# Talking-heads attention and a squared-ReLU FFN on one core: where the first batch's loads of v and w_in stand in the load queue

## The chip, the cores and the metric

The kernel runs on one core of a Trainium2 chip. The metric is the device time of one execution in microseconds (us), taken as the median over runs. Beside it there is one profiled execution, whose trace gives every instruction with its start, its length and what it waited for. The engines go by short names: PE is TensorE (PEld its weight loads), DVE is VectorE, ACT is ScalarE, POOL is GpSimd and SP is SyncE. SP computes nothing here; it issues transfers.

## The reference

Attention over 8 batches, 12 heads, 448 positions and a head dimension of 64, with the heads mixed before and after the softmax, and then a feed-forward net over all 3584 tokens:

```python
scores = scale * np.matmul(q, k.transpose(0, 1, 3, 2))
scores = np.einsum('bhij,hg->bgij', scores, w_pre)
scores = scores - np.max(scores, axis=-1, keepdims=True)
attn = np.exp(scores)
attn = attn / (np.sum(attn, axis=-1, keepdims=True) + 1e-09)
attn = np.einsum('bhij,hg->bgij', attn, w_post)
attn_out = np.matmul(attn, v)
x = attn_out.transpose(0, 2, 1, 3).reshape(B * S, H * D)      # 3584 x 768
out = np.maximum(x @ w_in, 0.0) ** 2 @ w_out                   # d_ff = 2048
```

The inputs are float32. They are turned into bfloat16 on their way into the core's memory, by the transfers that POOL issues.

## The kernel before

**The stages of a batch.** q and k come in by head and are transposed (line 491; the last 64 positions of q, the tails, at line 519). A score (line 629) is the product of one pair of heads with one of four blocks of rows: block 0 holds the tails, blocks 1 to 3 hold 128 rows each. The scores are cast into one of two buffers `snat`, in turn (lines 395 and 397). Mixing the heads needs them in another layout, with ten positions times twelve heads on the partitions, so SP issues a relayout (`move`, line 658), a transfer from `snat` to a small tile `sch`. In the first batch some relayouts carry three chunks at once (`triple`, line 607) into tiles that lie in `osb` and `h2`, which the feed-forward net needs only later (`tri`, line 387); two chunks share a smaller tile `schl`.

A chunk is then: mix with w_pre (line 753, or 749 with three matmuls for a chunk of a triple), row maximum on DVE (758), exponential with its sum on ACT (761), reciprocal (767), scaled w_post on POOL (770, `wq`), mix back and transpose (777), and a copy into `atb`. There are 45 chunks to a batch, 360 in all. The product with v (817) fills the rows of x; two batches make a unit's columns for the feed-forward net (870 with w_in, 883 ReLU, 886 square, 902 with w_out, 917 and 926 out).

**The order of the work.** The order of the instructions on every engine is written once, by a planner in the kernel (`Planner`, line 101). Each operation has a priority: chunk n has priority n, and its score and relayout have n less `AHEAD` (lines 636 and 670). The planner walks a model of the engines and of two transfer queues, "LOAD" for what POOL issues and "DMA" for what SP issues, and emits what is ready with the smallest priority. On the chip each engine then runs its instructions in this order and waits only for what the data needs. The planner lets a load be issued only when the seventh load before it has landed in its model (line 414). The constants AHEAD, LAST_W1, W2_AT and Q1_AT set places in the order.

**The loads of the first batch.** Ahead of the planner the kernel issues eight loads for k, the tails and q (LOADS0, line 53). Then, in `first_batch` (line 1022), POOL has a small copy, `hold` (line 1036), which reads a few columns of `snat` 0, and so waits until the six casts of the tails' scores are done. Behind it POOL issues v in two halves (`load_half`, line 1001) and six tiles of w_in (`load_w1`, line 987). The tiles of w_out and q and k of the next batch are issued at fixed chunks (lines 1049 to 1052). The product with v comes at 52 us and the first matmul with w_in at 57 us.

Of the kernel before, what the change touches and what calls it, by code (L numbers as in the profile page):

```python
# [10 lines left out]
BF16 = mybir.dt.bfloat16  # L11
F32 = mybir.dt.float32

B, H, S, D = 8, 12, 448, 64
DMODEL = H * D
DFF = 2048
NPAIR = H // 2
# [22 lines left out]
PIECE = NPAIR // 2  # L40
NE = 6
NSCH = 11
AHEAD = 7.4
FIFO = 50
ROWS, COLS = 1, 2
TURN = 95
# [27 lines left out]
TRI_IN = (0, 1)  # L74
W2_AT = [18, 21, 24, 27]
Q1_AT = [13, 16]
LAST_W1 = 4
TAIL0, Q0 = 19, 0.7
EARLY0 = 0

# [20 lines left out]
class Planner:  # L101
# [7 lines left out]
    def add(self, eng, ns, pri, fn, deps=(), lat=60, bank=None, frees=None, mode=0):  # L109
        op = Op(eng if isinstance(eng, dict) else {eng: ns}, lat, pri, fn, list(deps), bank, frees, mode)  # L110
        self.ops.append(op)
        return op
# [158 lines left out]
def kernel(  # L271
# [11 lines left out]
    nc = tc.nc  # L283
    P = nc.NUM_PARTITIONS

    sb = ctx.enter_context(tc.tile_pool(name="sb", bufs=1))
# [9 lines left out]
    vs = sb.tile([P_KEYS, H, NB, D], BF16, name="vs")  # L296
# [32 lines left out]
    def load_kv(dst, src, b, h0, h1):  # L329
        nc.gpsimd.dma_start(  # L330
            out=dst[:, h0:h1, :, :].rearrange("p h r d -> p h (r d)"),
            in_=src[b, h0:h1].rearrange("h (p r) d -> p h (r d)", r=NB),
        )
# [3 lines left out]
    for what in LOADS0:  # L337
# [15 lines left out]
        out=smask[:, :], in_=ident[0:KC, 0:KC].rearrange("p (s h) -> p s h", s=CI), axis=AX.X, op=ALU.add,  # L353
    )
    wmix = many(3, "wmix", [KC, P], BF16)
    for t_ in wmix:
# [4 lines left out]
        out=nmask[:, :], in0=smask[:, :], scalar1=-SCALE, scalar2=1.0, op0=ALU.mult, op1=ALU.mult,  # L361
# [3 lines left out]
        out=perm[:, :].rearrange("k (s x p) -> k s x p", s=CI, x=2),  # L365
        in_=ident[0:KC, 0:KC].rearrange("k (s p x) -> k s x p", s=CI, x=2),
    )
    for t_ in wmix[1:]:
        nc.vector.tensor_tensor(
            out=t_[:, 0:KC].rearrange("p (s h) -> p s h", s=CI),  # L370
# [4 lines left out]
        out=wback[:, :, :], in0=wpost_rep[:, :].unsqueeze(2).to_broadcast([KC, H, CI]),  # L375
# [5 lines left out]
        out=keep_m[:, :], in_=ident[0:KC, 0:KC].rearrange("p (s m g) -> p m s g", s=CI, m=3), axis=AX.XY, op=ALU.add,  # L381
# [19 lines left out]
    add = pl.add  # L401
# [12 lines left out]
    def load(rows, each, pri, fn, deps):  # L414
        if len(loads) >= 7:
            deps = list(deps) + [loads[-7]]
        op = add("POOL", 750, pri, fn, deps, lat=850)
        done = pl.moved("LOAD", rows, each[0], each[1], 0, [op], 1500)
        loads.append(done)
        return done  # L420

    q_in, k_in, v_in = {}, {}, {}
# [43 lines left out]
    score_ops, scopy = {}, {}  # L466
# [12 lines left out]
    def t_qk(b, p):  # L479
        i, at_ = slot_of(b, p)  # L480
        pri = b * NCHUNK - 19 + 1.5 * p
        old = used(b, p // PIECE)

        def turn(tag, at, ins, src, blocks, rows, dve, act, put):
            key = (tag, "t", b, p, blocks)

            def mms(slot):
                v_ = slot[:, :].bitcast(BF16)
                for r in range(blocks):
                    for x in range(2):  # L490
                        nc.tensor.transpose(  # L491
                            v_[64 * x:64 * x + 64, r * rows:(r + 1) * rows], src[:, 2 * p + x, r, :],
                            ident[0:rows, 0:rows],
                        )

            mm = add("PE", 200 + 55 * blocks, at, keep(key, mms), ins + old, lat=200, bank=key)
            ev = add({"DVE": dve, "ACT": act}, 0, at, lambda eng: put(eng, slots[key][:, :].bitcast(BF16)), [mm], frees=key)
            return mm, ev

        def put_k(eng, v_):  # L500
            copy(eng, kt[i][:, :, at_, :], v_[:, 0:S].rearrange("p (j c) -> p j c", c=P_KEYS))

        def put_q(eng, v_):
            copy(eng, qz[i][:, :, at_, :], v_[:, 0:NJ * P].rearrange("p (r c) -> p r c", c=P))

        mk, ek = turn("g", pri, [k_in[b, p // 2]], ks, NB, P_KEYS, 340, 460, put_k)
        at = pri + Q0 if b == 0 else pri + 3
        mq, eq = turn("g", at, [q_in[b, p // 2]], qs, NJ, P, 300, 420, put_q)
        ready[b, p] = [[ek]] + [[ek, eq]] * NJ
        got_op[b, p] = [mk, mq]  # L510

    def t_tail(b, g):
        key = ("f" if b == 0 else "g", "z", b, g)
        old = [score_ops[b - 1, 0, p] for p in range(3 * g, 3 * g + 3)] if b > 0 else []

        def mms(slot):
            v_ = slot[:, :].bitcast(BF16)
            for i in range(3):
                nc.tensor.transpose(v_[:, i * P:(i + 1) * P], qt[:, 3 * g + i, :], ident[:, :])

        def put(eng):
            copy(
                eng, zt[:, 3 * g:3 * g + 3, :].rearrange("p a c -> p (a c)"),
                slots[key][:, :].bitcast(BF16)[:, 0:3 * P],
            )

        pri = b * NCHUNK - (19 if b > 0 else TAIL0) + 3 * g
        mm = add("PE", 200, pri, keep(key, mms), [tail_in[b]] + old, lat=200, bank=key)
        ev = add({"DVE": 360, "ACT": 440}, 0, pri, put, [mm], frees=key)
        got_tail.setdefault(b, []).append(mm)  # L530
        for p in range(3 * g, 3 * g + 3):
            ready_tail[b, p] = ev
# [63 lines left out]
    def flip(b, r):  # L596
        return 1 - r if b == 0 and r < 2 and EARLY == 0 else r
# [4 lines left out]
    def store_of(b, r):  # L602
        return snat[flip(b, r) % 2]
# [9 lines left out]
    def groups(b, r):  # L613
        size = GROUP if b >= GROUP_AT and r > 0 else 1
        return [range(p, p + size) for p in range(0, NPAIR, size)]

    def score(b, r, group):
# [13 lines left out]
        first = [0, EARLY, C0[2], C0[3]][r] if b == 0 else C0[r]  # L631
        pri = b * NCHUNK + first - AHEAD - 0.6 - (0.7 if r == 0 else 1.4) * (NPAIR - p)
        n = b * (NJ + 1) + r - 2
# [19 lines left out]
    def block_of(c):  # L653
        r = sum(c >= c0 for c0 in C0) - 1
        return r, c - C0[r]
# [8 lines left out]
    def relayout(b, c):  # L664
# [6 lines left out]
        deps = list(scopy[b, r]) + (list(scopy[b, r - 1]) if r == 1 and cc == 0 else [])  # L671
        pri = n - AHEAD
        if r == 2 and cc == 0:
# [295 lines left out]
    started = add("POOL", int(1000 * at_) + 700, -100, lambda: None)  # L969
# [14 lines left out]
    w1_in, later = [], {}  # L984
    w2_in = [add("W2", 0, 0, lambda: None, lat=0) for i in range(4)]

    def load_w1(c2, pri, more=()):
        w1_in.append(load(16, (152, 148), pri, lambda: nc.gpsimd.dma_start(
            out=w1[c2][:, :], in_=moe_w_in[c2 * 128:(c2 + 1) * 128, 0:DFF], max_dma_last_dim=4096,
        ), [started, *more]))  # L990

    def load_w2(f4, n):
        f_, c_ = 8 * (f4 % 2), 384 * (f4 // 2)
# [3 lines left out]
        ), gate(n))  # L997
        done.next.append(w2_in[f4])
        w2_in[f4].left += 1

    def load_half(b, n, x, deps):
        h0 = x * H // 2
        v_in[b].append(load(42, (46, 58), n, lambda: load_kv(vs, v, b, h0, h0 + H // 2), deps))

    def load_v(b, n, deps):
        v_in[b] = [load(42, (46, 58), n, lambda h0=h0: load_kv(vs, v, b, h0, h0 + H // 2), deps) for h0 in (0, H // 2)]
# [14 lines left out]

    def first_batch():
        for i in range(NPAIR):
            if i == 0:
                v_in[0] = []
                for x in range(0):
                    load_half(0, -30 + x, x, [started])
        for p in range(NPAIR):
            t_qk(0, p)
        for g in range(2):  # L1030
            t_tail(0, g)
        for r in (1, 0):
            for p in groups(0, r):
                score(0, r, p)
        hold = sb.tile([P, NPAIR], BF16, name="hold")
        opened = add("POOL", 150, -6, lambda: nc.gpsimd.tensor_copy(
            out=hold[:, :], in_=store_of(0, 0)[:, 0:NPAIR, 0],
        ), scopy[0, 0])
        for x in range(0, 2):
            load_half(0, -5 + 0.1 * x, x, [opened])  # L1040
        for i in range(NPAIR):
            load_w1(i, -4 + 0.1 * i, [opened])
        for n, c in enumerate(ORDER0):
            if c in C0[2:]:
                for p in groups(0, block_of(c)[0]):
                    score(0, block_of(c)[0], p)
            relayout(0, c)
            chunk(0, c)
            if n in W2_AT:
                load_w2(W2_AT.index(n), n)  # L1050
            if n in Q1_AT:
                load_ahead(1, n, 6 * Q1_AT.index(n))
            if c == C0[1]:
                for g in range(3):
                    av(0, 0, g, 0, P_ROWS)
                unit(0, 0)
            if c == C0[2]:
                for g in range(3):
                    av(0, 0, g, P_ROWS, XA)
            if c == C0[3]:  # L1060
                for g in range(3):
                    av(0, 1, g, 0, P_ROWS)
                unit(0, 1)
        for g in range(3):
            av(0, 1, g, P_ROWS, XB)
        unit(0, 2)
# [78 lines left out]
```

## Time and profile before

| what | value |
|---|---|
| median of 3 runs | 590.29 us (589.7 to 591.21) |
| profiled execution | 591.14 us, of which 589.4 us are the span |
| PE busy | 565.2 us, 96% of the span |
| DVE / ACT / POOL busy | 82% / 80% / 55% |
| transfers issued by POOL and SP | 82.33 MB, mean 140 GB/s |
| w_in's six tiles, 512 KB each | median 21.8 us from issue to landing |
| granted TensorE clock, mean | 0.99 |

The span is the time between the first and the last instruction of the profiled execution. A line of the timeline gives the start, the length, the engine, the line in the kernel, what is written and read, how many instructions are merged, and in square brackets how long the engine stood idle before it and which instruction or transfer ended that. A window gives the busy time of each engine in a stretch, the granted clock (1.00 is full), the busy share of the core's sixteen DMA engines (over 1 where transfers overlap on an engine) and the bytes per second. A line of the chain of waits gives the start, the length and the work of one link; the chain is followed back from the last instruction.

### The profile page before, as it was taken

To read this page: it belongs to the slowest core of one execution; us is meant where nothing else is said; L and a number is where in the kernel's file an instruction comes from. 1 tells how busy PE (TensorE), PEld (TensorE's weight loads), DVE (VectorE), ACT (ScalarE), POOL (GpSimd) and SP (SyncE) were. 2 spreads that over 40 slices of the span, in tenths; PEclk is the share of its full clock that TensorE was granted. 3 is DMA by queue.
4 is the path that set the end of the run, shared out by engine and by line. 5 is a ranking of instruction groups with operands and counts; after the bars stand their busy time and mean duration, and the time that the engine had idled before them with its cause. 6 is when DMAs were issued, how large, how long until landed. Compare 5 with 4: busy or idle time off the path is not lost.

```text
span 589.4 us, 17018 instructions
## 1 busy us (share of the span) xinstructions
PE 565.2 (96%) x5751; PEld 403.8 (69%) x5751; DVE 486.1 (82%) x1240; ACT 471.3 (80%) x1239; POOL 326.2 (55%) x600
## 2 busy tenths in 40 slices
PE   5698999999999999999999999999999999999996
PEld 3346766776668766776867776876767866867783
DVE  4697999997798998999898898989798898989201
ACT  4597998888988988989898878888889988788330
POOL 4436647546667437744865538744865624735340
PEclk9897999999999999999999999999999999999999
DMA  8899969984596449964596639974497547322021
GB/s 95 181 217 215 211 135 166 181 168 130 104 203 147 131 127 164 187 152 135 102 187 168 144 90 169 183 142 140 89 175 186 136 107 144 105 83 78 2 53 55
DMA packets 132086, 82.33 MB, mean 140 GB/s; under 512 B 59582, under 2 KB 126286, under 8 KB 131998
## 3 DMA queue, kind: packets, MB, share of 16 engines
q1 hardware_dynamic: 85214, 58.42, 40.6%
q0 software_dynamic: 46784, 22.81, 30.6%
q8 instruction: 45, 0.74, 0.5%
q14 instruction: 43, 0.35, 0.2%
HBM read 45.62 MB, written 11.01 MB: 96 GB/s over the span
## 4 chain that ended last, share of the span: by engine, by line
PE 84%; ACT 5%; DMA 5%; issue 2%; DVE 1%; SPq 1%; POOL 1%; DVEq 0%; POOLq 0%; ACTq 0%
PE bank L902 24%; PE bank L870 24%; PE bank L777 12%; PE bank L753 10%; PE bank L817 7%; PE bank L629 6%; DMA sch<-snat 3%; ACT es L761 2%; DMA osb<-snat 1%; SPq L658 1%; ACT snat L397 1%; ACT hr L883 1%; DVE mn L758 1%; PE bank L491 1%; DMA qt<-in_q_dram 1%
## 5 line engine op out<-in xcount | busy, mean ns | idle before, releaser
L761 ACT ACTIVATE es<-bank,mn 120x448 bf16<-120x448 f32 x360 | 229.4, 643 | 40.2 <-DVE mn L758 35.1
L770 POOL TENSOR_SCALAR wq<-wback,rc 120x120 bf16<-120x120 f32 x360 | 130.5, 367 | 179.4 <-DVE rc L767 104.2
L758 DVE TENSOR_REDUCE mn<-bank 120x1 f32<-120x448 f32 x360 | 209.5, 609 | 8.4 <-PE bank L749 5.2
L902 PE MATMUL bank<-w,h 128*128 128x384 bf16 x896 | 174.3, 325 | 0.9 <-ACT es L761 0.5
L395 DVE CAST atb<-bank 112x480 bf16<-112x480 f32 (+3 forms) x227 | 142.1, 634 | 30.8 <-PE bank L777 27.8
L870 PE MATMUL bank<-xt,w 128*128 128x256 bf16 (+1 forms) x1632 | 164.5, 254 | 0.2
L870 PEld LDWEIGHTS <-w 128*128 128x128 bf16 x1632 | 135.7, 98 | 21.9 <-issue 2.3
L886 POOL TENSOR_TENSOR h<-hr 128x512 bf16<-128x512 f32 x112 | 116.2, 1039 | 54.7 <-ACT hr L883 52.2
L777 PEld LDWEIGHTS <-es 120*112 120x112 bf16 (+1 forms) x1440 | 116.9, 130 | 39.5 <-issue 8.1
L777 PE MATMUL bank<-wq,es 120*112 120x120 bf16 (+1 forms) x1440 | 129.6, 218 | 2.8 <-POOL wq L770 1.9
L902 PEld LDWEIGHTS <-h 128*128 128x128 bf16 x896 | 83.5, 97 | 55.1 <-issue 5.6
L753 PE MATMUL bank<-sch,wmix 120*128 120x448 bf16 x334 | 103.9, 355 | 1.3 <-DMA sch<-snat 0.9
L395 DVE CAST snat<-bank 128x448 bf16<-128x448 f32 x164 | 96.0, 612 | 6.3 <-PE bank L629 3.5
L397 ACT CAST atb<-bank 112x480 bf16<-112x480 f32 (+3 forms) x157 | 82.3, 540 | 15.7 <-PE bank L777 14.2
L883 ACT ACTIVATE hr<-bank 128x512 f32<-128x512 f32 x112 | 67.1, 599 | 31.0 <-PE bank L870 25.2
L397 ACT CAST snat<-bank 128x448 bf16<-128x448 f32 x172 | 84.9, 550 | 4.3 <-PE bank L629 3.2
L761 ACT ACTIVATION_READ_ACCUMULATOR es<-bank,mn 120x1 f32 x360 | 75.7, 210 | 0.0
L767 DVE RECIPROCAL rc<-sm 120x1 f32<-120x1 f32 x360 | 52.7, 153 | 14.4 <-ACT es L761 12.3
L917 DVE COPY osb<-bank 128x384 f32<-128x384 f32 x56 | 30.7, 549 | 31.6 <-PE bank L902 31.3
L753 PEld LDWEIGHTS <-wmix 120*128 120x128 bf16 x342 | 30.3, 98 | 19.0 <-issue 7.8
L629 PE MATMUL bank<-kt,qz 64*128 64x448 bf16 x288 | 42.6, 354 | 0.5 <-ACT atb L397 0.2
L817 PE MATMUL bank<-atb,vs 112*64 112x192 bf16 (+3 forms) x864 | 42.2, 255 | 0.5 <-ACT atb L397 0.5
(57 smaller groups left out, 248.6 us busy)
## 6 DMA issues: line engine op xcount, KB each, us to landing
sch<-snat SPq DMA_DIRECT2D x318, 105.0 KB
out_dram<-osb SPq DMA_DIRECT2D x23, 360.0 KB
vs<-in_v_dram POOLq DMA_DIRECT2D x16, 336.0 KB, 9.6
ks<-in_k_dram POOLq DMA_DIRECT2D x14, 336.0 KB, 10.0
qs<-in_q_dram POOLq DMA_DIRECT2D x14, 288.0 KB, 8.2
w<-in_moe_w_in_dram POOLq DMA_DIRECT2D x6, 512.0 KB, 21.8
w<-in_moe_w_out_dram POOLq DMA_DIRECT2D x4, 768.0 KB, 24.5
out_dram<-osb SPq DMA_DIRECT2D x8, 192.0 KB
```

What stands on the lines that cost most here:

```text
L395: nc.vector.tensor_copy(out=out_, in_=in_)
L397: nc.scalar.copy(out=out_, in_=in_)
L629: nc.tensor.matmul(slot[:, 0:S], lhsT=lhsT, rhs=kt[i][half, :, at_, :], start=True, stop=True)
L753: nc.tensor.matmul(slot[:, 0:S], lhsT=wm[0:rows, :], rhs=src[0:rows, :], start=True, stop=True,)
L758: nc.vector.tensor_reduce(out=mn[i][0:rows, :], in_=slots[mk][0:rows, 0:S], axis=AX.X, op=ALU.min)
L761: nc.scalar.activation(out=es[i][0:rows, 0:S], in_=slots[mk][0:rows, 0:S], func=ACT.Exp, scale=-1.0, bias=mn[i][0:rows, 0:1], accum_out=sm ...
L770: nc.gpsimd.tensor_scalar(out=wq[i][0:rows, :, 0:ns], in0=wback[0:rows, :, 0:ns], scalar1=rc[i][0:rows, 0:1], scalar2=1.0, op0=ALU.mult, o ...
L777: nc.tensor.matmul(slot[0:P_KEYS, jb * H * ns:(jb + 1) * H * ns], lhsT=es[i][0:rows, jb * P_KEYS:(jb + 1) * P_KEYS], rhs=wq[i][0:rows, :, ...
L817: nc.tensor.matmul(v_[64 * hh:64 * hh + 64, i, 0:x1 - x0], lhsT=vs[:, 2 * c2 + hh, jb, :], rhs=atb[half][:, jb, 2 * c2 + hh, x0:x1], start ...
L870: nc.tensor.matmul(slot[:, j * w:(j + 1) * w], lhsT=w1[c2][:, (f0 + j) * 128:(f0 + j + 1) * 128], rhs=xt[:, c2, a:z], start=(c2 == 0), sto ...
L886: nc.gpsimd.tensor_tensor(out=h2_[:, f0:f0 + nf, 0:w], in0=hr[gi % 2][:, :].rearrange("p (f c) -> p f c", f=nf), in1=hr[gi % 2][:, :].rear ...
L902: nc.tensor.matmul(slot[:, 0:384], lhsT=h2_[:, ft, mt * 128:(mt + 1) * 128], rhs=w2[:, ft, nt * 384:(nt + 1) * 384], start=(ft == 0), stop ...
```

## The change

Three things change in the first batch, and one constant changes for all batches.

The gate goes: the copy `hold` and the wait that it carries are taken out, and with it the argument through which loads waited for it. The six tiles of w_in and the two halves of v are made ready by `started` alone, the point at which POOL has issued q. Their order becomes one tile of w_in, both halves of v (`load_v`, which the other batches use already), and then the other five tiles: LAST_W1 says before which tile v stands. AHEAD goes from 7.4 to 7, which moves the priority of every score and relayout by 0.4 chunk.

```diff
-AHEAD = 7.4
+AHEAD = 7
...
-LAST_W1 = 4
+LAST_W1 = 1
...
-    def load_w1(c2, pri, more=()):
+    def load_w1(c2, pri):
         w1_in.append(load(16, (152, 148), pri, lambda: nc.gpsimd.dma_start(
             out=w1[c2][:, :], in_=moe_w_in[c2 * 128:(c2 + 1) * 128, 0:DFF], max_dma_last_dim=4096,
-        ), [started, *more]))
+        ), [started]))
...
-    def load_half(b, n, x, deps):
-        h0 = x * H // 2
-        v_in[b].append(load(42, (46, 58), n, lambda: load_kv(vs, v, b, h0, h0 + H // 2), deps))
...
     def first_batch():
         for i in range(NPAIR):
-            if i == 0:
-                v_in[0] = []
-                for x in range(0):
-                    load_half(0, -30 + x, x, [started])
+            if i == LAST_W1:
+                load_v(0, 0.1 + i, [started])
+            load_w1(i, 0.1 + i)
...
-        hold = sb.tile([P, NPAIR], BF16, name="hold")
-        opened = add("POOL", 150, -6, lambda: nc.gpsimd.tensor_copy(
-            out=hold[:, :], in_=store_of(0, 0)[:, 0:NPAIR, 0],
-        ), scopy[0, 0])
-        for x in range(0, 2):
-            load_half(0, -5 + 0.1 * x, x, [opened])
-        for i in range(NPAIR):
-            load_w1(i, -4 + 0.1 * i, [opened])
```

`load_v`, unchanged, issues the same two transfers as the two calls of `load_half`:

```python
def load_v(b, n, deps):
    v_in[b] = [load(42, (46, 58), n, lambda h0=h0: load_kv(vs, v, b, h0, h0 + H // 2), deps) for h0 in (0, H // 2)]
```

## The prediction

> **What bounds the kernel now.** I read the page's head first, then busy time and clock by windows, the timelines of SP, POOL, PE and DVE over the first 60 us, and the chain of waits. The page:
>
> ```profile
> span 589.4 us, 17018 instructions
> PE 565.2 (96%) x5751; PEld 403.8 (69%) x5751; DVE 486.1 (82%) x1240; ACT 471.3 (80%) x1239; POOL 326.2 (55%) x600
> ```
>
> TensorE (PE) is busy for 96% of the span, so a change far from it costs nothing. The windows show where the rest lies (columns: window, its length, busy time of PE, PEld, DVE, ACT and POOL, granted clock, DMA share, GB/s):
>
> ```profile
> 11.00:12.00 1.00, 1.00 (x18) 0.83 (x18) 1.00 (x4) 0.77 (x2) 0.00 (x0) 1.00 0.70 82
> 12.00:13.00 1.00, 1.00 (x8) 0.30 (x8) 0.81 (x3) 1.00 (x3) 0.00 (x0) 1.00 0.07 8
> 14.00:15.00 1.00, 1.00 (x18) 0.48 (x16) 0.57 (x2) 0.81 (x2) 0.00 (x0) 1.00 0.00 0
> 16.00:17.00 1.00, 0.96 (x7) 0.22 (x8) 1.00 (x5) 1.00 (x4) 1.00 (x2) 1.00 0.23 75
> 24.00:28.00 4.00, 3.67 (x15) 1.93 (x16) 2.01 (x4) 1.38 (x4) 0.36 (x1) 0.57 1.16 271
> 48.00:56.00 8.00, 7.09 (x112) 5.46 (x113) 5.08 (x13) 4.92 (x15) 4.67 (x8) 0.57 1.38 207
> 100.00:540.00 440.00, 438.10 (x4387) 315.81 (x4386) 393.26 (x997) 377.42 (x1004) 253.99 (x476) 1.00 0.73 144
> ```
>
> From 100 to 540 us PE idles for 1.9 us in all. The time to be won or lost by the loads is in the first 60 us. There the DMA lies idle from about 11.7 to 16.2 us, and the granted clock is 0.57 in two stretches. This is the start, by engine:
>
> ```profile
> 15.20 0.19 POOL L1036 COPY hold<-snat 128x6 bf16<-128x6 bf16 x1 [6.87 <-ACT qz L397]
> 15.70 1.59 POOL L330 DMA_DIRECT2D vs<-in_v_dram  x2 [0.30 <-issue]
> 17.27 4.33 POOL L988 DMA_DIRECT2D w<-in_moe_w_in_dram  x6
> 15.15 1.82 SPq L658 DMA_DIRECT2D osb<-snat  x2
> 38.60 0.76 SPq L658 DMA_DIRECT2D schl<-snat  x1
> 19.56 1.86 PE L749 MATMUL bank<-osb,wtri_all 120*128 120x448 bf16 x9 [2.15 <-DMA osb<-snat]
> 24.33 2.31 PE L749 MATMUL bank<-osb,wtri_all 120*128 120x448 bf16 x6 [2.91 <-DMA osb<-snat]
> 25.56 0.62 DVE L758 TENSOR_REDUCE mn<-bank 120x1 f32<-120x448 f32 x1 [3.04 <-PE bank L749]
> 45.65 0.10 PEld L753 LDWEIGHTS <-wmix 96*128 96x128 bf16 x1 [0.75 <-DMA schl<-snat]
> ```
>
> POOL waits until 15.20 for the tails' scores and then issues the eight loads. The first relayout leaves SP at 15.15 and releases chunks 0 to 2 at 19.56, 4.4 us later. The second leaves at 16.05 and releases chunks 3 to 5 only at 24.33, 8.3 us later, because v and w_in came between. VectorE (DVE) idles 3.04 us for it. The last line is the nearest row to what the change makes: the schl relayout, 63 KB, leaves SP at 38.60 when SP's earlier relayouts have landed and tiles of w_in still wait in the load queue. It lands at 45.65, after 7.05 us.
>
> **The change, part by part.**
>
> *The gate goes.* One POOL copy of 0.19 us goes; POOL was idle for 6.87 us before it, so this is worth nothing.
>
> *Eight loads move forward.* They are two for v (1.59 us of POOL together) and six for w_in (4.33 us), 5.9 us of issue. POOL's last work before them ends at 8.34, so they issue from 8.34 to about 14.3 instead of 15.70 to 21.6. On POOL they pass only the gate; the first work behind them is the first wq at 22.35, so POOL costs nothing. On the DMA they now stand ahead of the three relayouts that SP issues at 15.15, 16.05 and 17.02, where they stood beside or behind them. The loads flow from the end of q, 11.7 us, instead of 16.5 to 17: about 5 us of transfer is moved into idle DMA time. One tile of w_in lands about every 2.3 us when little else runs (34.6, then 36.9, in the landings before), half of v took about 2 us at the 160 to 188 GB/s that k and q had. So when the first relayout starts to move at 16.2, one tile and half of v are through, and half of v and five tiles lie ahead.
>
> *The first relayout.* No row shows it behind a full queue, so I bound it. Below: no added wait. Above: all of the schl row's 7.05 us as wait. Between: the second relayout, 8.3 us against 4.4 us, 3.9 us of wait. The schl row, less 4.4 us for a larger transfer with nothing ahead, gives at least 2.65 us. I take 3.9, the nearest in size and place. Chunks 0 to 2 then start at 23.5 instead of 19.56.
>
> The Trainium skill speaks against this step: its page "DMA: Bandwidth & Descriptors", section "Queues, rings and completion order", says that each DMA engine goes round between the queues it has work for and changes at packet boundaries, so a relayout would not stand behind a whole queue of loads. The 7.05 us for 63 KB look longer than such sharing, but do not exclude it. By that page the sum below would be 2.1 - 1.6 = +0.5 us instead of +2.1.
>
> *What that delays.* PE idles from 17.4 to 23.5. After the 2.9 us idle before 24.33 the clock was 0.57 and six matmuls took 2.31 us, 0.385 each; nine of them take 3.5 us, to 27.0. The second relayout stands behind the first in SP's queue; the large ones landed some 1.6 to 2 us apart (24.3 to 32.3 for the next four and three small ones), so it is there by 25.5 and no longer late. Chunks 3 to 5 then run at full clock, nine matmuls of 0.24 us (0.73 us per three later on) and 0.6 us of the matmuls between them, to 29.7. Before, they were through at 28.1. So the start loses **+1.6 us**, with ends of 0 (the first relayout comes early enough for chunk 3) and +4.7 (7.05 us of wait: 3.1 more). The later relayouts of this block follow the same queue: the one issued at 23.88 and landed at 32.34 stands on the chain of waits, and comes 1 to 2 us later, within this term.
>
> ```profile
> 23.88 8.46 DMA osb<-snat
> 41.90 9.38 DMA sch<-snat
> ```
>
> *Earlier end of w_in.* The last tile landed at 48.6 (issued 20.8, 27.8 us) and now lands near 43.6. Its consumer, the first hidden layer, starts at 56.9 both ways. What gains are the relayouts from 38.6 to 45, of which one stands on the chain with 9.38 us. PE itself waited for them twice, 0.9 us in all, at 49.3 and 51.3; VectorE was busy without a gap from 44 to 52, so more than that is not theirs to give. The next batch's q and k still come at 43.5, so I take half, **-0.5 us** (ends 0 and -0.9).
>
> *AHEAD 7.4 to 7.* Scores and relayouts of every batch get a due time 0.4 chunk later: 589.4 us over 360 chunks is 1.64 us per chunk, so 0.65 us. From 100 to 560 us the waits for relayouts are these (total, times, longest):
>
> ```profile
> PEld L753 <- DMA sch<-snat: 1.1, 3, 0.4
> ```
>
> Three loads of weights come late, and each could be 0.65 us later: +2.0 us above. Below, a new order could take away the 1.9 us that PE idles from 100 to 540: -1.9. I take half of the upper end, **+1.0 us**, since the waits that exist can only lengthen and a gain needs luck in the order. LAST_W1 only names the place of v.
>
> The sum is +1.6 - 0.5 + 1.0 = +2.1 us. The profiled execution had a span of 589.4 us and 591.14 us in all, 1.74 around the span; it would become 591.5 and 593.2. The median of the three runs is 590.29, 0.85 under the profiled execution, and becomes 592.4.
>
> **The rivals.** A difference of 0.3%, 1.8 us, is about what a measurement of this kernel can tell from no change.
>
> *Faster: the second clock slump goes.* From 48 to 56 us PE is busy 7.09 us at a mean clock of 0.57; at full clock that work is some 4.1 us, 3.0 less. The slump follows idle PE from 44 to 52 (5.73 of 8 us busy). If the first relayout shares the DMA at once, its 2 us of movement double at most: it lands by 21.6, its nine matmuls are through before 24.33, and the start costs nothing. If the relayouts near 40 then land early enough to keep PE busy, 0.9 + 3.0 go: 586.4 us. It decides when chunks 0 to 2 start before about 21.6 and the clock holds past 48. For it: the DMA idle at 12 to 16 us is truly unused. Against: VectorE is full from 44 to 52, so PE waits there anyhow. The page named above would take its first half so: its round between the queues is that sharing.
>
> *Hidden anyway.* The start costs 0, the later waits give 0.5 to 0.9, the order 0 to +1.0: 589.4 to 590.8. For it: the second relayout already set the start, and its landing need not move.
>
> *The load queue holds more.* If the wait is the whole 7.05 us, the start costs +4.7, and with the upper end for AHEAD the sum is 4.7 + 2.0 = +6.7: 597.0. For it: five whole tiles of w_in lie ahead, and near 38.6 three or four did. Against: at 16.2 half of the near queue is v, whose parts are smaller.
>
> *AHEAD decides.* -1.9 with a start of 0 to +0.5 gives 588.4 to 588.9; the upper side lies within the other cases.
>
> **How the numbers follow.** Forecast with its neighbourhood (590.8 to 594.5) 0.45; the deeper queue (594.5 to 597) 0.17; hidden anyway 0.13; the clock slump gone 0.17; a lucky order 0.08. Faster by over 0.3% (under 588.5) are the last two, 0.25. Within 0.3% are the hidden case and the lower edge of the forecast's neighbourhood, 0.13 + 0.06 = 0.19. Slower is the rest of it, 0.39 + 0.17 = 0.56. The likeliest is 592.4. The range reaches from 587.5, just above the full price of the slump, to 597.0; about 0.1 is left out on each side. The forecast's own range is 590.8 to 594.5.
>
> **What would show it.** Right: POOL issues loads from about 8.3 us without a wait; the DMA moves over 150 GB/s from 12 to 15 us; the first nine matmuls of chunks 0 to 2 start at 22.5 to 25 us, released by the osb relayout; the wait before chunk 3 is gone and its reduction comes at 26.5 to 28 us; the last tile of w_in lands near 44; from 100 to 540 us PE idles 2 to 4 us. Wrong: chunks 0 to 2 start before 21 us (the loads don't hold a relayout up), or the clock stays at 1.0 from 48 to 56, or PE's busy time from 100 to 540 moves by more than 2 us, which would make the order written by the planner, not the loads, the cause.

## The result and the profile after

The changed kernel takes 595.66 us (median of six runs, 594.08 to 597.23) against 590.79 for the kernel before (six runs): a ratio of 1.0081, 95% interval 1.0058 to 1.0104. That is 4.9 us slower. The forecast was slower by 2.1 us. Here and below, a difference in us is the ratio minus one, times the time of the kernel before that was measured beside it. The head of the page after:

```profile
span 594.4 us, 17010 instructions
PE 562.9 (95%) x5751; PEld 401.9 (68%) x5751; DVE 486.7 (82%) x1242; ACT 473.6 (80%) x1243; POOL 322.9 (54%) x593
```

PE's busy time fell by 2.3 us and the span rose by 5.0, so PE idles 31.5 us instead of 24.2. The windows of the kernel after (window, length, busy time of PE, PEld, DVE, ACT, POOL, granted clock, DMA share, GB/s) say where:

```profile
12.00:15.00 3.00, 3.00 (x46) 1.45 (x45) 2.95 (x8) 3.00 (x8) 2.08 (x3) 1.00 1.18 199
19.00:22.00 3.00, 0.00 (x0) 0.00 (x0) 0.00 (x0) 0.00 (x0) 0.00 (x0) 0.50 1.10 276
38.00:42.00 4.00, 3.71 (x28) 1.63 (x28) 4.00 (x11) 3.39 (x8) 0.73 (x2) 1.00 0.02 4
48.00:56.00 8.00, 5.65 (x73) 4.32 (x73) 5.70 (x15) 5.32 (x18) 4.75 (x9) 0.82 1.35 208
100.00:540.00 440.00, 433.50 (x4362) 312.12 (x4361) 392.36 (x996) 379.10 (x1005) 250.10 (x466) 1.00 0.74 144
```

The DMA is now busy from 12 to 15 us, as it was to be, and empty from 38 to 42, where the kernel before was still loading w_in. But the last line holds most of the loss: from 100 to 540 us, far behind the loads, PE idles 6.5 us instead of 1.9. The timeline of the start, by engine:

```profile
8.24 0.76 POOL L988 DMA_DIRECT2D w<-in_moe_w_in_dram  x1
9.00 1.57 POOL L330 DMA_DIRECT2D vs<-in_v_dram  x2
10.54 3.54 POOL L988 DMA_DIRECT2D w<-in_moe_w_in_dram  x5
14.23 1.82 SPq L658 DMA_DIRECT2D osb<-snat  x2
22.16 4.81 PE L749 MATMUL bank<-osb,wtri_all 120*128 120x448 bf16 x15 [5.67 <-DMA osb<-snat]
27.23 0.73 PE L749 MATMUL bank<-osb,wtri_all 120*128 120x448 bf16 x3
23.48 0.62 DVE L758 TENSOR_REDUCE mn<-bank 120x1 f32<-120x448 f32 x1 [5.79 <-PE bank L749]
```

The first relayout leaves SP at 14.23 and releases PE at 22.16, 7.9 us later instead of 4.4. In return the second wait, before chunk 3, is gone: fifteen matmuls run in one piece. Chunks 0 to 5 are through at 27.96 (27.23 + 0.73), before 28.10.

To see where the kernel falls behind I compared the starts of the products with v, which come twice a batch. After against before they are 0.8 us late in the first batch (52.97 against 52.17), 0.3 at 73 us, 2.8 at 92, 1.8 at 121, 1.7 at 158, 1.5 at 189, 3.6 at 290, 4.4 at 320, 3.4 at 491. So the first batch, which the loads belong to, costs under 1 us in these two profiles. The rest is lost later. The points place the loss only roughly, because the two orders put other work between these products: from 121 to 158 us PE is busy for 33.7 us in the kernel after, and for 35.6 between the same two products before. PE's waits from 100 to 540 us show one large hole (line that waited, what ended the wait, total, times, longest); before, no single wait was over 0.5 us:

```profile
PE bank L777 <- DVE snat L395: 2.6, 1, 2.6
PE bank L753 <- DVE snat L395: 1.5, 4, 0.6
PE bank L777 <- ACT snat L397: 0.7, 1, 0.7
```

### The profile page after: what moved, and what is told of

It reads as the page before. It is cut to its first block, busy times and chain, and to the rows that moved or that the text cites. A ratio compares the mean times of both kernels' runs of the same rounds, so it can differ in the third digit from the quotient of the medians.

```text
span 594.4 us, 17010 instructions
## 1 busy us (share of the span) xinstructions
PE 562.9 (95%) x5751; PEld 401.9 (68%) x5751; DVE 486.7 (82%) x1242; ACT 473.6 (80%) x1243; POOL 322.9 (54%) x593
## 4 chain that ended last, share of the span: by engine, by line
PE 79%; DVE 8%; DMA 5%; ACT 3%; issue 2%; POOL 1%; SPq 1%; DVEq 0%; ACTq 0%; POOLq 0%
PE bank L870 22%; PE bank L902 22%; PE bank L777 12%; PE bank L753 10%; PE bank L817 7%; PE bank L629 5%; DVE mn L758 3%; DMA sch<-snat 3%; DVE snat L395 2%; DVE atb L395 1%; DMA osb<-snat 1%; ACT es L761 1%; ACT snat L397 1%; DVE rc L767 1%; PE bank L749 1%
## 5 line engine op out<-in xcount | busy, mean ns | idle before, releaser
L395 DVE CAST atb<-bank 112x480 bf16<-112x480 f32 (+2 forms) x221 | 137.4, 633 | 28.2 <-PE bank L777 26.2
L777 PEld LDWEIGHTS <-es 120*112 120x112 bf16 (+1 forms) x1440 | 113.7, 130 | 44.3 <-issue 10.3
L777 PE MATMUL bank<-wq,es 120*112 120x120 bf16 (+1 forms) x1440 | 126.4, 217 | 8.8 <-POOL wq L770 4.4
L395 DVE CAST snat<-bank 128x448 bf16<-128x448 f32 x171 | 100.2, 614 | 8.3 <-DMA out_dram<-osb 3.8
L397 ACT CAST atb<-bank 112x480 bf16<-112x480 f32 (+3 forms) x163 | 85.8, 542 | 8.2 <-PE bank L777 7.4
L397 ACT CAST snat<-bank 128x448 bf16<-128x448 f32 x165 | 81.5, 545 | 10.4 <-DMA out_dram<-osb 3.5
```

The source lines that it names most:

```text
L395: nc.vector.tensor_copy(out=out_, in_=in_)
L397: nc.scalar.copy(out=out_, in_=in_)
L777: nc.tensor.matmul(slot[0:P_KEYS, jb * H * ns:(jb + 1) * H * ns], lhsT=es[i][0:rows, jb * P_KEYS:(jb + 1) * P_KEYS], rhs=wq[i][0:rows, :, ...
```

## The experiments

Two things differ between the kernels on the chip: when the eight loads are issued, and the order of the instructions of all batches, which the planner writes anew when its input changes (its list of operations, its constants or the figures of its model). My theory after the result was that the loads cost about 1 us and the order about 4. The rival was that the late first relayout is carried through to the end. A second question was whether the order is worse because AHEAD is shorter.

### The loads alone, and the order alone

The first kernel keeps the order of before and opens the gate, by letting its copy read a tile that is always there:

```diff
-            out=hold[:, :], in_=store_of(0, 0)[:, 0:NPAIR, 0],
+            out=hold[:, :], in_=ident[:, 0:NPAIR],
```

> The kernel before with one instruction changed: the POOL copy hold reads the identity instead of the scores, so it waits for nothing and the eight loads (v first, then w_in) issue from about 8.3 us. The order of every engine is that of the kernel before. Theory of the order (the loads cost about 1 us, the order that the planner wrote for the other batches about 4 us): +0 to +1.5 us against before. Theory of the loads (the late first relayout is carried through to the end): +3 to +5 us.

The second keeps the order of the changed kernel and puts the gate back. The eight loads (`issues` lists the loads as the kernel asks for them) are taken out of the planner's list and emitted behind a copy that reads the tails' scores:

```diff
-        for op, args in pl.run():
-            op.fn(*args)
+        held, casts = [], list(scopy[0, 0])
+        hold = sb.tile([P, NPAIR], BF16, name="hold")
+        for op, args in pl.run():
+            if casts and op in issues[:8]:
+                held.append(op)
+                continue
+            op.fn(*args)
+            if op in casts:
+                casts.remove(op)
+                if not casts:
+                    nc.gpsimd.tensor_copy(out=hold[:, :], in_=store_of(0, 0)[:, 0:NPAIR, 0])
+                    for x in held:
+                        x.fn()
```

> The changed kernel, instruction by instruction in its own order, with the gate put back: a POOL copy that reads the tails' scores stands before the eight loads. Theory of the order: +3 to +5 us against before, hardly less than the changed kernel's +4.9. Theory of the loads: 0 to +1 us.

| order | gate | ratio to before (95%) | difference |
|---|---|---|---|
| of before | shut (before) | 1 | 0 |
| of before | open | 1.0025 (1.0007 to 1.0044) | +1.5 us |
| of after | shut | 1.0084 (1.0071 to 1.0097) | +5.0 us |
| of after | open (after) | 1.0081 (1.0058 to 1.0104) | +4.9 us |

The theory of the order holds, with both results at the upper end of what it expected, and its rival falls. The moved loads alone cost 1.5 us (0.4 to 2.6), and in the new order the gate makes no difference to the time. The timeline and a window of the first kernel (old order, gate open):

```profile
22.70 5.44 PE L749 MATMUL bank<-osb,wtri_all 120*128 120x448 bf16 x15 [5.33 <-DMA osb<-snat]
28.19 0.73 PE L749 MATMUL bank<-osb,wtri_all 120*128 120x448 bf16 x3
48.00:56.00 8.00, 5.76 (x134) 4.78 (x134) 6.62 (x19) 6.61 (x21) 6.04 (x13) 1.00 1.36 196
100.00:540.00 440.00, 437.81 (x4389) 315.89 (x4388) 392.61 (x997) 376.58 (x1002) 253.72 (x474) 1.00 0.74 144
```

With the loads early in the old order, PE starts chunk 0 3.1 us later than before and is through chunk 5 at 28.92, 0.8 us later. The clock from 48 to 56 us is 1.00 instead of 0.57, and from 100 to 540 PE idles 2.2 us, about as before. And of the second kernel (new order, gate shut):

```profile
19.36 1.86 PE L749 MATMUL bank<-osb,wtri_all 120*128 120x448 bf16 x9 [1.91 <-DMA osb<-snat]
25.65 2.42 PE L749 MATMUL bank<-osb,wtri_all 120*128 120x448 bf16 x6 [4.44 <-DMA osb<-snat]
145.48 0.63 PE L777 MATMUL bank<-wq,es 120*112 120x120 bf16 x8 [2.89 <-DVE snat L395]
100.00:540.00 440.00, 434.73 (x4372) 312.97 (x4370) 393.21 (x998) 379.57 (x1008) 251.81 (x470) 1.00 0.74 145
```

Here the first relayout is on time, chunk 0 starts at 19.36, and the hole near 140 us is there all the same, 2.89 us long, with 5.3 us of idle PE from 100 to 540. It belongs to the order. Chunks 3 to 5 wait longer here (4.44 us) and are through only at 29.60, but the time is that of the kernel after.

### Which part of the edit writes the slower order

> The kernel before with AHEAD 7 in place of 7.4, gate and loads as before. If the constant is what makes the later batches slower: +3 to +5 us, with PE idle 5 to 7 us from 100 to 540 us. Theory of the loads: within 1 us of before.

> The changed kernel with AHEAD back at 7.4: the loads moved, gate gone. If the constant is the cause: 0 to +1.5 us against before. If the moved loads are, on the chip or through the order that the planner writes around them: +3 to +5 us.

The edit is one constant in each: AHEAD = 7 in the kernel before, AHEAD = 7.4 in the changed one. AHEAD alone gives 1.0059 (1.0039 to 1.0079), +3.5 us; the moved loads with AHEAD 7.4 give 1.0109 (1.0086 to 1.0132), +6.4 us, more than either theory allowed; its interval overlaps that of the whole change. So the parts don't add up, and neither is the cause by itself. That led to a third theory: the order of before is a good one among many, and any change to the planner's input loses it.

Three kernels test that. The first changes nothing but a figure of the planner's model, the length that it assumes for the gate's copy:

```diff
-        opened = add("POOL", 150, -6, lambda: nc.gpsimd.tensor_copy(
+        opened = add("POOL", 600, -6, lambda: nc.gpsimd.tensor_copy(
```

> The kernel before with one figure of the planner's model changed, the length that it assumes for the gate's copy, 600 ns in place of 150. No instruction, load, gate or constant differs; only the order that the planner writes does. If the order of the kernel before is a lucky one, which any change to the planner's input loses: +2 to +5 us. If the loss comes from what AHEAD or the load order mean: within 1 us of before.

The other two set AHEAD to 7.3 and 7.5:

> The kernel before with AHEAD 7.3. If a shorter lead is the cost, a quarter of the loss at AHEAD 7 (+3.5 us): about +1 us. If any other order is: +2 to +5 us, no less than at 7.

> The kernel before with AHEAD 7.5, a longer lead. If a shorter lead is the cost: no loss, 0 to -1 us. If any other order is: +2 to +5 us.

| kernel | ratio to before (95%) | difference | PE idle, 100 to 540 us |
|---|---|---|---|
| assumed length 600 | 1.0258 (1.0232 to 1.0284) | +15.2 us | 10.0 us |
| AHEAD 7.3 | 1.0133 (1.0094 to 1.0172) | +7.9 us | 5.5 us |
| AHEAD 7.5 | 1.0128 (1.0092 to 1.0164) | +7.6 us | 6.0 us |
| AHEAD 7 | 1.0059 (1.0039 to 1.0079) | +3.5 us | 2.2 us |

A figure that stands for nothing on the chip costs three times as much as the whole change. A longer and a shorter lead cost the same, and 7 costs less than 7.3. So what AHEAD means as lead time does not show; what shows is a new order. The third theory holds, and its three tests lost more than the 2 to 5 us that it expected. All seven changed inputs that were run here, the change itself among them, are slower by 3.5 to 15.2 us. The window of the kernel with the assumed length of 600:

```profile
100.00:540.00 440.00, 429.99 (x4326) 307.39 (x4326) 388.10 (x984) 373.35 (x987) 251.79 (x464) 0.99 0.74 144
```

The loss does not lie in this stretch alone. In the same profile PE idles 4.0 us from 60 to 80 us (0.4 before), and the granted clock is 0.978 on average (0.990 before). One load moved in that order too: POOL issues the sixth tile of w_in at 23.02, behind two wq, instead of 20.84.

With AHEAD 7 the idle time of 5 to 7 us that was expected is not there: 2.2 us. The profile is of one of its shorter executions, 593.15 us against a median of 594.87; whether that is the reason is not shown.

The changed kernel with AHEAD 7.1:

> The changed kernel with AHEAD 7.1. If the changed kernel too stands at a picked order, a neighbour is slower than it: +6 to +12 us against before. If orders scatter round the changed kernel's time: +2 to +7 us.

It gave 1.0114 (1.0073 to 1.0155), +6.7 us, which lies in both ranges. Whether the changed kernel's own order is a picked one stays open.

### What in the new order makes the hole near 140 us

The timelines of SP, DVE and PE in the kernel after:

```profile
132.24 1.28 SPq L573 DMA_TRANSPOSE qz<-qn  x1
133.62 6.92 SPq L658 DMA_DIRECT2D sch<-snat  x8
142.24 1.16 DVE L395 CAST snat<-bank 128x448 bf16<-128x448 f32 x2 [3.77 <-DMA out_dram<-osb]
142.92 0.63 PE L777 MATMUL bank<-wq,es 120*112 120x120 bf16 x8 [2.62 <-DVE snat L395]
```

SP issues eight relayouts of one block from 133.62 to 140.54. The casts of a later block write into the same score buffer. They start at 142.24, 1.7 us after the last of these issues, and PE goes on only then. The profile names a store to `out`. I took the relayouts for the true cause: SP issues them late because transposes stand ahead of them. In the kernel before, though, both transposes stand ahead of eight relayouts too, and the last relayout leaves 2.7 us sooner:

```profile
129.29 1.54 SPq L573 DMA_TRANSPOSE qz<-qn  x1
130.93 6.93 SPq L658 DMA_DIRECT2D sch<-snat  x8
```

There the casts that follow wait 1.27 us, until 139.57, and PE waits nowhere from 100 to 540 us for more than 0.5 us. So the transposes are not what the new order added, and why SP comes later to these relayouts in it stays open; the tests only ask whether their late end makes the hole. The first test moved both transposes of batch 2's second half of k and q behind the relayouts (`turns` holds SP's two instructions for them):

> The changed kernel in its own order, but for two instructions of SP: the transposes of batch 2's second half of k and q (near 130 us) move behind the nine relayouts that follow. If those relayouts, late in SP's queue, are what holds the casts of the next block and PE for 2.6 us near 140 us: the last of them is issued some 3 us sooner, that idle time falls under 0.5 us, and the kernel is 2 to 3 us faster than the changed one, +2 to +3 us against before, unless the transposes come too late in their turn. If the idle time has another cause: it stays, and the time stays at +4.9 us.

```diff
-        for op, args in pl.run():
-            op.fn(*args)
+        order = pl.run()
+        late = turns[2, 1]
+        at = max(i for i, (op, _) in enumerate(order) if op in late)
+        moves = [i for i, (op, _) in enumerate(order) if i > at and op.eng == "SP"]
+        for i, (op, args) in enumerate(order):
+            if op not in late:
+                op.fn(*args)
+            if i == moves[7]:
+                for x in late:
+                    x.fn()
```

It gave 1.0178 (1.0134 to 1.0222), slower still by 5.7 us than the kernel after. The transposed k came too late, as the timeline of PE shows:

```profile
143.20 0.93 PE L629 MATMUL bank<-kt,zt 128*128 128x448 bf16 x2 [5.64 <-DMA kt<-kn]
```

The test was spoilt for its question, but shows another thing: this hole was carried to the end nearly in full. Its products with v are 1.5 us later than the kernel after's at 121 us, ahead of the hole, then 8.1 at 158 us, 7.9 at 189, 7.6 at 491, and the span is 7.5 longer. So the hole brought 6.6 us, and 6.0 of them are left at the end. The second test moved the transpose of q alone (`late = turns[2, 1][1:]`):

> The changed kernel in its own order, but for one instruction of SP: of the two transposes near 130 us only that of q, which is needed later than that of k, moves behind the eight relayouts that follow (with both moved, PE waited 5.6 us for k, and the test was spoilt). If the relayouts late in SP's queue hold the casts and with them PE for 2.6 us near 140 us: the last one is issued 1.3 to 1.4 us sooner, the wait shrinks to 1.0 to 1.6 us and the time by about as much, to +3 to +4 us against before. If the wait has another cause: it stays at 2.6 us and the time at +4.9 us.

```profile
131.47 7.81 SPq L658 DMA_DIRECT2D sch<-snat  x9
141.35 1.16 DVE L395 CAST snat<-bank 128x448 bf16<-128x448 f32 x2 [2.16 <-DMA sch<-snat]
142.03 0.63 PE L777 MATMUL bank<-wq,es 120*112 120x120 bf16 x8 [1.01 <-DVE snat L395]
```

The wait of PE fell from 2.62 to 1.01 us and that of the cast from 3.77 to 2.16, now put down to a relayout by name. The store to `out` did not hold the casts: it left SP no sooner than in the kernel after (140.76 against 140.63), and the casts came 0.9 us sooner. Against the kernel after, the products with v go from 0.7 us late at 121 us to 0.9 us early at 158. So one instruction of SP, moved by eight places, is worth 1.6 us across the hole in the trace, and the hole is shown there to hang on when SP has issued its last relayout; 1.0 us of it is left. The time is 1.0055 (1.0026 to 1.0083), +3.3 us against before, inside what was expected, but its interval overlaps that of the kernel after, so the gain in time is not clear of noise. Where the rest of the 4.9 us comes from in the new order was not followed.

### What the first relayout pays, and whether early loads can be had for nothing

Two kernels keep the order of before and issue only two tiles, or one tile, of w_in ahead of the gate (`issues[2:4]` or `issues[2:3]`, the first tiles of w_in, emitted before the planner's list):

```diff
+        for op in issues[2:4]:
+            op.fn()
         for op, args in pl.run():
-            op.fn(*args)
+            if op not in issues[2:4]:
+                op.fn(*args)
```

> The kernel before, in its own order on every engine, but for two of the six tiles of w_in, which POOL issues ahead of the gate instead of behind it: 2 x 2.3 us of transfer for the idle DMA between 11.7 and 16.2 us, so that nothing stands ahead of the first relayout. If the price of the moved loads is the late first relayout, this has none of it: chunks 0 to 2 start at 19 to 20 us, the last tile of w_in lands some 4 us sooner, 0 to -1.5 us against before. If early loads cost in another way (more work near 40 us collides): +0.5 to +1.5 us, as with all eight loads early (+1.5).

> The kernel before, in its own order, with one tile of w_in issued ahead of the gate (two gave a ratio of 0.9986, 0.9967 to 1.0004). If what early loads cost is the wait of the first relayout, one tile is through by 14 us and costs none: chunks 0 to 2 start at 19.2 to 19.7 us instead of 20.3, -0.5 to -1.5 us against before. If nothing but chance spoke for the two tiles: within 0.5 us of before.

Two tiles give 0.9986 (0.9967 to 1.0004), one tile 0.9998 (0.9970 to 1.0025). Neither is told from no change, so no version here beats the kernel before. Two tiles lie inside their first range, but its premise failed: the second tile landed at 18.86, so it still stood ahead of the first relayout, and chunk 0 started at 20.30 instead of 19 to 20. With one tile chunk 0 started early, at 18.69, but the time is that of the second case, chance. The starts of chunk 0, first with two tiles, then with one:

```profile
20.30 3.49 PE L749 MATMUL bank<-osb,wtri_all 120*128 120x448 bf16 x9 [3.29 <-DMA osb<-snat]
```

```profile
18.69 3.52 PE L749 MATMUL bank<-osb,wtri_all 120*128 120x448 bf16 x9 [2.42 <-DMA osb<-snat]
```

The first relayout left SP at 14.75 and 14.01 here, so it took 5.55 and 4.68 us, beside 4.4 with nothing ahead and 7.6 with all eight loads ahead in the same order (15.10 to 22.70).

## Why the prediction was right in direction and short in size

**The first relayout: right.** The step took 3.9 us of added wait, between 0 and 7.05. In the old order it was 3.2 us (7.6 against 4.4), in the kernel after 3.5 (7.9), or 3.8 against the new order with the gate shut (15.19 to 19.36). Chunk 0 started at 22.16, a little under the range given, because SP issued the relayout 0.9 us sooner in that execution. The order is not the reason: with the gate shut the new order issued it at 15.19, and with one tile early the old order issued it at 14.01. Two smaller readings were a little off: before, the first tiles of w_in landed at 34.53 and 36.98, 2.45 us apart and not 2.3, and SP's queue moved its first packet at 16.7 and not at 16.2.

The rule of the Trainium skill that was weighed there ("DMA: Bandwidth & Descriptors", "Queues, rings and completion order": the engines go round between queues at packet boundaries) would, by the prediction's estimate, have doubled the relayout's 2 us of movement at most. The wait grew with what stood ahead, 0.3, 1.15 and 3.2 us for one tile, two tiles and all eight loads, and the last is more than that doubling. By that page's rule alone the size is not explained. The trace lists a transfer piece by piece, as packets, and shows by queue where the wait lies. In the kernel after, SP's queue moved nothing until 18.7 us, 4.5 us after the issue (1.5 before); then the queues did share, with 178 packets of SP's queue beside 206 of the loads' from 19 to 22 us. The first 315 KB of SP's queue, the relayout's size, took 2.5 us instead of 1.8. So about 3 of the 3.5 us lie ahead of its first packet and 0.7 in the sharing; why the first packet comes so late stays open.

**What it delays: half the size.** The step gave +1.6 us. The clock did halve (0.50 from 19 us on) and the wait before chunk 3 did go, but chunks 3 to 5 were through at 28.92 in the old order, +0.8, and at 27.96 in the kernel after, not at 29.7.

**Earlier end of w_in: more than forecast.** The last tile, issued at 13.3, landed 24.5 us later, at 37.8 instead of 43.6. The gain of 0.5 to 0.9 us for the relayouts behind it is there with the old order, where PE's waits for them in the first 60 us are gone; its waits for wq there rose from 0.7 to 3.2 us. In the kernel after the waits for the relayouts rose from 0.9 to 2.3 us, since SP issued those relayouts at 41.05 instead of 38.60, in another order.

The two terms that belong to the loads sum to +1.1 us. The run with the loads alone measured +1.5 (0.4 to 2.6). They agree in the sum; one by one, the second step was half its size and the third came out otherwise than forecast, so part of the agreement is luck.

**AHEAD 7.4 to 7: the step that failed.** The prediction took the constant for 0.65 us of lead and gave it +1.0 us, with ends of -1.9 and +2.0. The runs show that it is not a lead that matters: 7.3 and 7.5 are slower by the same, and a figure with no meaning on the chip costs 15 us. What the step should have priced is a new order of every engine for all eight batches, and the edit of the loads brings such an order too, by itself +6.4 us with AHEAD at 7.4. The new order measured +5.0 us with the gate shut. The prediction allowed for a gain only by a lucky order, and did not ask whether the order of before was the lucky one, though its 1.9 us of idle PE in 440 us could have raised the question. It did name the sign: PE's busy time from 100 to 540 us was to move by less than 2 us, or else the order would be the cause. It moved by 4.6 (438.10 to 433.50).

**The rivals.** The clock slump did go, in the profile with the old order (1.00 from 48 to 56 us). That kernel is still 1.5 us slower than before, so the second half of that rival did not bring the time it promised. Its profiled execution, 589.0 us of span, is one of its shorter ones and had a mean clock of 0.993 (0.990 in the profile before). In it PE idles 1.6 us more in the first 60 us (17.1 against 15.5), which the higher clock made up for. Other executions had a lower clock: at 0.987 the four of that kernel took 592.3 to 594.0 us, the eight of the kernel before 590.0 to 591.8. So the 1.5 us are probably that idle time; a profile of such an execution, which would show it, was not taken. The whole queue's 7.05 us of wait did not come. The measured 595.66 us lies above the forecast's own range and inside that rival's, 594.5 to 597.0, but it got there by another path, and that is luck. "AHEAD decides" came nearest, through the order and on the other side than the one priced.

## What to carry to other kernels

Where a planner writes the whole order, test an edit with the order held fixed, or the order with the edit held fixed, before giving its cost to the edit: here the edit was worth 1.5 us and the new order that it brought 5. If PE idles hardly at all in the long middle, as in these 1.9 us of 440, take that order for a find that a change of the planner's input can lose, as all seven did here, and forecast the loss. Ask too what a full load queue does to the first transfer behind it that an engine waits for: here eight loads ahead delayed the first relayout by 3.2 us, two by 1.15 and one by 0.3, though issuing fewer of them early brought no gain that could be measured.

## What the runs showed of the hardware that I had not expected

A wait of 5.6 us on PE at 143 us (the first test of the hole) was carried to the end of the kernel almost unchanged. With the clock at 0.50 from 143 to 147 us, after the wait, it put the kernel 6.6 us further behind, and 6.0 of these were left at the end, though DVE, ACT and POOL idled for 11%, 13% and 41% of the time from 143 to 491 us. The granted clock fell to 0.5 about 2.5 us after PE went idle at 16.5 us in the kernel after, and stayed there for almost 4 us of work after it started again at 22.16:

```profile
18.00:19.00 1.00, 0.00 (x0) 0.00 (x0) 0.00 (x0) 0.00 (x0) 0.00 (x0) 1.00 1.10 185
19.00:20.00 1.00, 0.00 (x0) 0.00 (x0) 0.00 (x0) 0.00 (x0) 0.00 (x0) 0.51 1.11 275
25.00:26.00 1.00, 1.00 (x4) 0.41 (x3) 0.51 (x2) 0.72 (x2) 0.00 (x0) 0.57 1.12 279
```
